# Folding w_out in four column groups, 32-row tiles for the last keys of the small attention, six staging slots

## The chip, the cores and the metric

One core of one Trainium2 chip runs the kernel. The metric is device time in microseconds, the median of several runs. Most runs of this kernel lie within 0.3% of each other.

## The reference, cut to what matters

Three stages follow each other. The sizes are 4 batches, 8 heads, 576 positions, head size 64; 2304 tokens of 512; 1536 hidden columns; 8 experts with 4 slots each.

```
q_d, k_d, v_d = means over 4 neighbouring positions          # 144 positions
out  = repeat(softmax_attention(q_d, k_d, v_d), 4) + local_attention(q, k, v)   # |i - j| < 4
x    = out as (2304, 512)
x    = (x @ w_a) * (x @ w_b) @ w_out                          # w_a, w_b: 512 x 1536, w_out: 1536 x 512
logits = x @ phi                                              # phi: 512 x 32
slots  = softmax(logits, over tokens).T @ x                   # 32 x 512
y[e]   = relu(slots[e] @ w1[e]) @ w2[e]                       # 8 experts
return softmax(logits, over slots) @ y
```

w_a, w_b and w_out arrive as float64 words and become float32 on the chip.

## The kernel before, in words

The x of the second stage is never multiplied by w_out token by token. The kernel **folds** w_out into phi first (w_out @ phi, 1536 x 32) and takes logits from the gated product; w_out itself is applied later to the 32 slots. The attention is worked out batch by batch: the **small attention** over the 144 pooled positions (`plan_datt`), and the local attention in pairs of 116 positions (`plan_pair`), whose output is split in a high and a low part (`xhi`, `xlo`) for the **main matmuls** (`plan_unit`, line 1086). These go over five groups of 384 or 512 tokens; a group has 12 units, a unit two halves (w_a and w_b), and a half 12 matmuls: four blocks of 128 rows, three products each.

**Weights.** `plan_piece` brings one piece of w_a, w_b or w_out (512 KB of words) into a staging slot, makes its low bits (`clow`), magnitude (`mag`) and bits (`bits`), and for w_a and w_b the high and low parts (`chi`, `clo`). Two pieces make one weight tile, which serves two units. The first `FIRST` = 20 pieces use the four slots named `st`, the later ones the two slots named `sw`. The `st` slots are taken out of the 24 places named `w8`, and all are given back when the last of the `FIRST` pieces is done. A weight tile takes two `w8` places.

**Folding.** A piece of w_out.T holds 128 of the 512 columns of w_out and 512 hidden rows. `omm` (line 947) folds two pieces in one task: a piece is one matmul of 32 x 512 into its own 32 partitions of `ps`. After four pieces, `e1` copies the 128 x 512 result to SBUF and `e2` (line 1046) adds the four groups of 32 partitions and turns them, in four matmuls; `e3` copies them to `wpr`. That is done for three blocks of hidden rows (fc = 0, 1, 2).

**Small attention.** `dscore`, `dmax`, `dexp`, `dnorm` and `dptr` (lines 673, 686, 701, 293, 733 to 740) make the transposed weights in three parts: two parts of four heads with the first 128 keys, and one with the last 16 rows. The last 16 keys of all eight heads are kept in one tile, `dvr`, of 8 x 16 = 128 rows; a head's columns in it are zero outside its own 16 rows. `dout(n)` (line 779) makes the output of four heads: for each of two column halves two matmuls over the first 128 keys, then two over all 128 rows of `dvr`. `doev` copies it, and `pv` and `xadd` of the batch's pairs need it.

**Order.** The programme of every engine is written out by hand: `ORDER` lists all tasks, `OTHER` those that go to their second engine. A task is a closure with one or a few instructions. Engines take their tasks strictly in that order, so an engine that waits holds up all that stands behind it. Loads are all issued by SP, in order too. Idle times of TensorE that the order foresees are filled with matmuls on constants (lines 347 and 352).

Of the kernel before, what the change touches and what calls it, by code (L numbers as in the profile page):

```python
# [9 lines left out]
F32 = mybir.dt.float32  # L10
# [238 lines left out]
def tile_attn_glu_softmoe(  # L249
# [16 lines left out]
    nc = tc.nc  # L266
    ctx.enter_context(tc.manual_schedule())
    P = Plan(dict(CAPS))
    add = P.add
# [338 lines left out]
    def plan_datt(b):  # L608
# [163 lines left out]
        def dout(n):  # L772
            pt = X.pop(("pt", b, n))
            X["do", b, n] = ps = psum((128, 2, 144))
            for hl in range(2):
                for part in range(2):
                    for j in range(2):
                        h = 4 * n + 2 * j + hl
                        nc.tensor.matmul(  # L779
                            out=ps[j * 64:j * 64 + 64, hl, :],  # L780
                            lhsT=(X["dvr", b] if part else X["dv", b])[:, h, :],
                            rhs=X["pr", b] if part else pt[:, 2 * j + hl, :],
                            start=(part == 0),
                            stop=(part == 1),
                        )
            if n == 0:
                done_with(PT_AT[b], X.pop(("ptr", b)))
            if n == 1:
                X.pop(("dv", b))
                X.pop(("dvr", b))  # L790
                X.pop(("pr", b))
# [37 lines left out]
        for n in (2, 0, 1):  # L829
# [6 lines left out]
            if n == 1:  # L836
# [8 lines left out]
                alt=("V", 0.85 if n < 2 else 0.8, WT["norm"]), lk=0.0, gi=2,  # L845
# [14 lines left out]
            T["pt", b, n] = t6  # L860
        for n in range(2):
            o = pr + 0.2 + 0.1 * n
            t7 = add(
                "PE", 1.05, lambda n=n: dout(n), [T["pt", b, n]] + tb + vv + T["xd", b] + T.get(("dout", b), []), o - 40,
                acq=("ps",) if n else ("ps", "xd"), rel=("dpt", "dv", "dvr", "dpr") if n else (PT_AT[b],), part="128x64",
            )
            T.setdefault(("dout", b), []).append(t7)
            T["xd", b].append(
                add("A", 0.4, lambda n=n: doev(n), [t7] + T["xd", b], o, rel=("ps",))
            )  # L870

# [30 lines left out]
    def plan_piece(n, key):  # L902
# [39 lines left out]
        def omm():  # L942

            if ("wp", fc) not in X:
                X["wp", fc] = psum((128, 512))
            for x in range(m - OQ + 1, m + 1):
                nc.tensor.matmul(  # L947
                    out=X["wp", fc][x * 32:x * 32 + 32, :], lhsT=phis[:, x, :],
                    rhs=words(X["raw", (fc, x)])[0].bitcast(F32), start=True, stop=True,
                )  # L950
# [16 lines left out]
        if isw:  # L967
            t5 = add(
                "A", 0.57, chi, [t4, T.get(("chi",) + key[:3]), T.get("chi0") if m == 0 else None], o - 0.01, acq=("w8", "w8") if m == 0 else (), alt=("G", 0.62, WT["chi"])
            )  # L970
            T["chi", *key[:3]] = t5
            if m == 0:
                T["chi0"] = t5
            t7 = add("G", 1.3, clo, [t5], o - 1, alt=("V", 0.63, WT["clo"]), lk=0.0)
            part.append(t7)
            T.setdefault(("w",) + key[:3], []).append(t7)
        else:
            T.setdefault(("ocv", fc), []).append(t4)
            if m % OQ == OQ - 1:
                if m == OQ - 1:  # L980
                    T["lg", fc] = add("N", 0.0, lambda: None, [t4], -100, acq=("lg", "ps"), lat=0.0)
                t7 = add("PE", 0.95, omm, T["ocv", fc][m - OQ + 1:] + [t_phi, T["lg", fc]], o - 20, part="128x32")
                T.setdefault(("omm", fc), []).append(t7)
                for x in range(m - OQ + 1, m):
                    T["conv"].append(add("N", 0.0, lambda x=x: X[where].append(X.pop(("raw", (fc, x)))), [t7], 0, rel=(where,), lat=0.0))
                part += [t7]
            else:
                return
# [48 lines left out]
    def plan_wprime(fc):  # L1037
        def e1():
            X["wT", fc] = sb(at, "dpt", (128, 4, 144)).rearrange("p a b -> p (a b)")[:, 0:512]
            nc.scalar.copy(out=X["wT", fc], in_=X.pop(("wp", fc)))  # L1040

        def e2():
            X["wq", fc] = ps = psum((128, 4, 32))
            wT = X.pop(("wT", fc))
            for fi in range(4):
                nc.tensor.matmul(
                    out=ps[:, fi, :], lhsT=wT[:, fi * 128:fi * 128 + 128], rhs=rep32, start=True, stop=True
                )
# [7 lines left out]
        t = add("A", 0.58, e1, T["omm", fc], -5, acq=("dpt",), rel=("ps", "lg"))  # L1056
        t = add("PE", 0.92, e2, [t, t_cst], -45, acq=("ps",), rel=("dpt",))
# [563 lines left out]
OQ = 2  # L1621
# [6 lines left out]
FIRST = 20  # L1628
# [3 lines left out]
def cpr(c):  # L1632
# [122 lines left out]
```

## Time and profile before

| | |
|---|---|
| median of 3 runs | 488.15 us (487.72 to 488.18) |
| profiled execution | 489.66 us, of which its span 487.9 us |
| PE busy | 470.3 us (96%) |
| DVE, ACT, POOL busy | 270.0, 153.3, 118.7 us |
| main matmuls, line 1086 | 1440, 56% of the chain that ended last |
| granted TensorE clock | 0.994 |
| DMA | 84.26 MB, mean 173 GB/s |

PE is TensorE, DVE is VectorE, ACT is ScalarE, POOL is GpSimd, SP issues the loads. The span is the time from the first to the last instruction; the profiled execution's own time is 1.8 us longer. PE is nearly always busy, so a PE instruction that is left out shortens the span, unless something else is late. In the first 80 us some of the busy time is filler; in the last 15 us the output leaves.

### The profile page before, as it was taken

Reading aid. Unit: us, or ns where it says so; the run is one execution under the profiler, and the core shown is the slowest. Engines: PE = TensorE matmul, PEld = TensorE weight load, DVE = VectorE, ACT = ScalarE, POOL = GpSimd, SP = SyncE. Lnnn points to the kernel's source line nnn. Section 1 sums busy time; section 2 is a strip of 40 time slices with the busy share of each in tenths; the row PEclk is TensorE's granted clock in tenths of the full one; section 3 lists DMA queues with packets and bytes.
Section 4 is the critical chain, followed back from the end, with each engine's and each line's share of the span. In section 5 each row is a group of like instructions: output and inputs, shape, how many; then the busy total and the mean of one; then the engine's idle time right before and its main releaser. Section 6 shows DMA issues by size and latency. Waiting matters only on the chain.

```text
span 487.9 us, 11280 instructions
## 1 busy us (share of the span) xinstructions
PE 470.3 (96%) x4702; PEld 366.5 (75%) x4702; DVE 270.0 (55%) x561; ACT 153.3 (31%) x403; POOL 118.7 (24%) x181
## 2 busy tenths in 40 slices
PE   8989988999999999999999999999999999999992
PEld 4678978987777687778788777778878889853471
DVE  4889899675654943686534237623332735660131
ACT  2876666342233521220152201302030301130142
POOL 6887787110540210633130002200000000010000
PEclk9999999999999999999999999999999999999997
DMA  8987862344444100413001010033223778999997
GB/s 297 385 279 238 294 192 93 124 172 155 165 153 154 46 0 27 131 64 125 3 22 45 1 39 28 24 118 119 87 86 130 263 257 313 401 364 411 407 406 287
DMA packets 30402, 84.26 MB, mean 173 GB/s; under 512 B 3472, under 2 KB 4240, under 8 KB 30352
## 3 DMA queue, kind: packets, MB, share of 16 engines
q1 hardware_dynamic: 30352, 83.54, 47.9%
q8 instruction: 37, 0.61, 0.5%
q14 instruction: 13, 0.11, 0.1%
HBM read 78.81 MB, written 4.72 MB: 171 GB/s over the span
## 4 chain that ended last, share of the span: by engine, by line
PE 83%; ACT 0%; DVE 0%; DVEq 0%; issue 0%
PE ps L1086 56%; PE ps L1246 3%; PE ps L1508 3%; PE ps L1455 3%; PE ps L1111 3%; PE ps L530 2%; PE ps L779 1%; PE ps L516 1%; PE ps L947 1%; PE ps L472 1%; PE ps L1547 1%; PE ps L673 1%; PE ps L1163 1%; PE ps L352 1%; PE ps L733 1%; PE ps L1414 1%
## 5 line engine op out<-in xcount | busy, mean ns | idle before, releaser
L1086 PE MATMUL ps<-x,w 128*128 128x512 f32 (+1 forms) x1440 | 307.5, 371 | 1.0 <-DVE x L293 0.9
L1086 PEld LDWEIGHTS ps<-x,w 128*128 128x128 f32 x1440 | 260.2, 188 | 46.1 <-issue 9.1
L1101 DVE TENSOR_TENSOR gr<-a,ps 128x512 f32<-128x512 f32 (+1 forms) x60 | 37.8, 629 | 82.4 <-PE ps L1086 73.8
L288 ACT COPY a<-ps 128x512 f32<-128x512 f32 (+1 forms) x35 | 19.3, 556 | 89.9 <-PE ps L1086 89.9
L293 POOL TENSOR_TENSOR x<-xn,x 128x464 fp32r<-128x464 f32 (+4 forms) x16 | 17.4, 1094 | 89.2 <-ACT x L288 83.7
L1119 DVE STREAM_TRANSPOSE gr<-gr 128x1024 f32<-128x1024 f32 (+2 forms) x31 | 33.1, 1086 | 9.2 <-PE ps L1111 9.2
L1233 POOL TENSOR_TENSOR cn<-lc,cs 128x128 f32<-128x128 f32 (+1 forms) x5 | 1.9, 377 | 119.3 <-DVE cs L1230 74.9
L290 DVE COPY a<-ps 128x384 f32<-128x384 f32 (+1 forms) x25 | 15.1, 603 | 20.7 <-PE ps L1086 20.7
L541 DVE TENSOR_TENSOR xn<-ps,xd 128x232 f32<-128x232 f32 (+1 forms) x40 | 13.8, 388 | 13.6 <-PE ps L530 13.4
L347 PE MATMUL ps<-acc 128*128 128x512 f32 (+2 forms) x44 | 16.8, 513 | 3.5 <-POOL acc L340 2.2
L293 POOL TENSOR_TENSOR w<-w,w 128x512 fp32r<-128x512 f32 x14 | 19.1, 1373 | 0.6
L293 POOL TENSOR_TENSOR e<-e,mx 128x512 f32<-128x512 f32 x12 | 12.5, 1045 | 27.0 <-DVE mx L506 27.0
L499 ACT ACTIVATE e<-e 128x512 f32<-128x512 f32 x20 | 12.6, 632 | 17.9 <-DVE e L492 17.8
L480 DVE TENSOR_REDUCE mx<-ps 128x4 f32<-128x256 f32 x40 | 14.7, 415 | 6.1 <-PE ps L472 6.1
L430 POOL TENSOR_TENSOR dT<-dT,qk 128x116 f32<-128x116 f32 (+1 forms) x34 | 17.4, 512 | 2.7
L288 ACT CAST x<-xn 128x464 fp32r<-128x464 f32 (+5 forms) x17 | 8.9, 532 | 27.7 <-DVE xn L541 27.7
L530 PEld LDWEIGHTS ps<-e,bv 64*64 64x64 f32 x640 | 12.4, 133 | 5.6 <-issue 3.4
L1246 PE MATMUL ps<-gr,lgs 32*32 32x384 f32 x576 | 16.4, 491 | 0.0
L892 ACT ACTIVATE ps<-w8x 128x512 f32<-128x512 f32 x12 | 7.6, 638 | 26.7 <-DVE a L290 13.3
L892 ACT ACTIVATE ps<-sw 128x512 f32<-128x512 f32 x16 | 10.1, 631 | 17.0 <-DMA sw<-in_w_outt_dram 11.1
L347 PEld LDWEIGHTS ps<-acc 128*128 128x128 f32 x44 | 8.4, 208 | 9.3 <-issue 6.6
L492 DVE TENSOR_TENSOR e<-ps,mx 128x256 f32<-128x256 f32 x40 | 14.7, 416 | 0.0
(205 smaller groups left out, 589.5 us busy)
## 6 DMA issues: line engine op xcount, KB each, us to landing
w<-in_moe_w_dram SPq DMA_DIRECT2D x33, 512.0 KB, 7.2
qk<-in_qk_dram SPq DMA_DIRECT2D x17, 480.0 KB, 4.8
sw<-in_w_outt_dram SPq DMA_DIRECT2D x12, 512.0 KB, 4.2
w8x<-in_moe_w_out_dram SPq DMA_DIRECT2D x12, 512.0 KB, 3.9
w<-in_moe_w_a_dram SPq DMA_DIRECT2D x10, 512.0 KB, 5.6
w<-in_moe_w_b_dram SPq DMA_DIRECT2D x10, 512.0 KB, 4.9
bv<-in_vw_dram SPq DMA_DIRECT2D x20, 256.0 KB, 3.8
w8x<-in_moe_w_dram SPq DMA_DIRECT2D x10, 512.0 KB, 10.3
```

The costliest lines, as they stand in the source:

```text
L288: nc.scalar.copy(out=out, in_=in_)
L290: (nc.vector if e == "V" else nc.gpsimd).tensor_copy(out=out, in_=in_)
L293: (nc.vector if e == "V" else nc.gpsimd).tensor_tensor(**a)
L347: nc.tensor.matmul(out=X["warm"][:, 0:128 * w], lhsT=x[:, 0:128], rhs=x[:, 0:128 * w], start=True, stop=True)
L430: nc.gpsimd.tensor_tensor(out=dst, in0=dst, in1=one[r], op=ALU.add)
L480: nc.vector.tensor_reduce(out=mx[:, hl], in_=X["s", n, hl], op=ALU.max, axis=AX.X)
L530: nc.tensor.matmul(out=pss[hl][o:o + 64, hq // 2, bi * w:bi * w + w], lhsT=v[r, bi, hq, :], rhs=pt[r, hq, 1 + bi * 64:1 + bi * 64 + w], st ...
L892: nc.scalar.activation(out=f, in_=words(raw)[0].bitcast(F32), func=ACTF.Prelu, scale=2.0 ** -112, alpha=-(2.0 ** 32))
L1086: nc.tensor.matmul(out=ps, lhsT=X["w", fc, ab, fi // 2, wi][:, fi % 2, hq, :], rhs=X[x, g][:, hq, :], start=(hq == 0 and m == 0), stop=(hq ...
L1101: nc.vector.tensor_tensor(out=X["g", g][:, k, :], in0=X.pop(("a", g, k)), in1=X.pop(("mm", g, k, 1)), op=ALU.mult)
L1119: nc.vector.transpose(out=t, in_=t)
L1246: nc.tensor.matmul(out=ps[q][o:o + 32, :], lhsT=d[r, b, :], rhs=g[r, :, b * 32:b * 32 + 32], start=(b < 4), stop=(b >= gt // 32 - 4),)
```

## The change

`omm` folds one piece in a task of its own: four matmuls of 128 columns, one to each group of 32 partitions, and the four pieces of a block are added up in `ps` while they come. `e1` then copies 128 x 128, and `e2` is one transpose. `dout` of a batch is one task instead of two, and its second parts take only the 32 rows of `dvr` and `pr` that two heads share. The `st` slots are six and `FIRST` is 18. `ORDER` and `OTHER` are new throughout (1328 tasks instead of 1326).

```
-        def dout(n):
-            pt = X.pop(("pt", b, n))
-            X["do", b, n] = ps = psum((128, 2, 144))
+        def dout():
+            pts = [X.pop(("pt", b, n)) for n in range(2)]
+            pss = [psum((128, 2, 144)) for _ in range(2)]
+            v, w, q = X.pop(("dv", b)), X.pop(("dvr", b)), X.pop(("pr", b))
             for hl in range(2):
                 for part in range(2):
-                    for j in range(2):
-                        h = 4 * n + 2 * j + hl
-                        nc.tensor.matmul(
-                            out=ps[j * 64:j * 64 + 64, hl, :],
-                            lhsT=(X["dvr", b] if part else X["dv", b])[:, h, :],
-                            rhs=X["pr", b] if part else pt[:, 2 * j + hl, :],
...
+                    for n in range(2):
+                        X["do", b, n] = pss[n]
+                        for j in range(2):
+                            h = 4 * n + 2 * j + hl
+                            r = slice(64 * n + 32 * j, 64 * n + 32 * j + 32)
+                            nc.tensor.matmul(
+                                out=pss[n][j * 64:j * 64 + 64, hl, :], lhsT=w[r, h, :] if part else v[:, h, :],
+                                rhs=q[r, :] if part else pts[n][:, 2 * j + hl, :], start=(part == 0), stop=(part == 1),
+                            )
...
         def omm():
-            if ("wp", fc) not in X:
-                X["wp", fc] = psum((128, 512))
-            for x in range(m - OQ + 1, m + 1):
+            if m == 0:
+                X["wp", fc] = psum((128, 128))
+            w = words(X["raw", key])[0].bitcast(F32)
+            for y in range(4):
                 nc.tensor.matmul(
-                    out=X["wp", fc][x * 32:x * 32 + 32, :], lhsT=phis[:, x, :],
-                    rhs=words(X["raw", (fc, x)])[0].bitcast(F32), start=True, stop=True,
+                    out=X["wp", fc][y * 32:y * 32 + 32, :], lhsT=phis[:, m, :], rhs=w[:, y * 128:y * 128 + 128],
+                    start=(m == 0), stop=(m == 3),
                 )
...
         def e2():
             X["wq", fc] = ps = psum((128, 4, 32))
-            wT = X.pop(("wT", fc))
-            for fi in range(4):
-                nc.tensor.matmul(
-                    out=ps[:, fi, :], lhsT=wT[:, fi * 128:fi * 128 + 128], rhs=rep32, start=True, stop=True
-                )
+            nc.tensor.transpose(out=ps.rearrange("p a b -> p (a b)"), in_=X.pop(("wT", fc)), identity=ident)
...
-OQ = 2
-FIRST = 20
+FIRST = 18
-    ps=8, un=2, lg=2, st=4, sw=2, ...
+    ps=8, un=2, lg=2, st=6, sw=2, ...
```

**Start-up, the queue of loads (SP).** `qk` and `x` are the queries and keys of the pairs (`x` where they lie in spare room), `cst` and `xn` constants, `w_87` and so on the staging slots, `sw` the two late slots, `bv` and `gr` values. Before:

```order
L413 DMA qk<-in_qk_dram 128x960
L370 DMA cst<-const_dram 128x269
L367 DMA xn<-const_dram 128x192
L413 DMA qk<-in_qk_dram 128x960
L413 DMA x<-in_qk_dram 128x960 x2
L913 DMA w_87<-in_moe_w_a_dram 128x2x256
L413 DMA x<-in_qk_dram 128x960
L652 DMA bv<-in_vr_dram 128x256
```

In the change:

```order
L413 DMA qk<-in_qk_dram 128x960 x2
L367 DMA xn<-const_dram 128x192
L370 DMA cst<-const_dram 128x269
L413 DMA x<-in_qk_dram 128x960 x3
L904 DMA w_143<-in_moe_w_a_dram 128x2x256
L652 DMA bv<-in_vr_dram 128x256
```

All five pairs of the first batch are now loaded ahead of the first piece of weights.

**The folding on PE, at the first block's end.** L1086 (now L1068) are main matmuls, L947 (L939) is `omm`, L1046 (L1030) is `e2`, L462 and L516 belong to the local attention. Before:

```order
L1086 MATMUL ps<-x,w_866 128x512 x2
L1086 MATMUL ps<-x,w_867 128x512
L1046 MATMUL ps<-cst,dpt 128x32 x4
L947 MATMUL ps<-sw,phis 32x512 x2
L462 LDWEIGHTS eyeb
```

In the change:

```order
L516 MATMUL ps<-cst,e 128x128 x4
L1030 MATMUL ps<-cst,dpt 128x128
L939 MATMUL ps<-sw,phis 32x128 x4
L1068 MATMUL ps<-x,w_997 128x512 x2
L1068 MATMUL ps<-x,w_998 128x512
```

A task of two matmuls of 512 columns is now one of four of 128 columns, and there are twelve of them instead of six.

**The small attention's output on PE, batch 1.** `gr` and `dpt` hold the transposed weights of the first and the second four heads. Before, the first of two tasks:

```order
L516 MATMUL ps<-cst,e 128x128 x8
L779 MATMUL ps<-gr,dv 64x144 x2
L779 MATMUL ps<-dpr,dvr 64x144 x2
L779 MATMUL ps<-gr,dv 64x144 x2
L779 MATMUL ps<-dpr,dvr 64x144 x2
L1086 MATMUL ps<-x,w_1024 128x384 x2
```

In the change, the only one:

```order
L516 MATMUL ps<-cst,e 128x128 x4
L784 MATMUL ps<-gr,dv 64x144 x2
L784 MATMUL ps<-dpt,dv 64x144 x2
L784 MATMUL ps<-dpr,dvr 64x144 x4
L784 MATMUL ps<-gr,dv 64x144 x2
L784 MATMUL ps<-dpt,dv 64x144 x2
L784 MATMUL ps<-dpr,dvr 64x144 x4
L1068 MATMUL ps<-x,w_1058 128x384 x2
```

The 16 matmuls of a batch stand together, in four runs that change between 128 and 32 rows.

## Rows read from the trace of the kernel before

**Rows 1.** Windows: us, busy time (instructions) of PE, PEld, DVE, ACT, POOL; clock, DMA share, GB/s.

```profile
60.00:80.00 20.00, 17.07 (x108) 15.76 (x107) 19.29 (x35) 13.80 (x37) 15.01 (x18) 1.00 0.42 133
80.00:100.00 20.00, 20.00 (x223) 17.95 (x224) 13.65 (x28) 8.11 (x22) 6.21 (x8) 1.00 0.46 145
...
440.00:470.00 30.00, 30.00 (x429) 14.60 (x429) 2.68 (x9) 4.41 (x10) 0.00 (x0) 1.00 1.03 408
```

**Rows 2.** Timeline of PE at start-up: start, length, what, idle before and its releaser.

```profile
40.23 2.18 PE L1086 MATMUL ps<-x,w 128*128 128x384 f32 x11 [0.91 <-DVE x L293]
...
63.21 0.44 PE L733 MATMUL ps<-cst,gr 128*128 128x128 f32 x2 [1.56 <-POOL gr L293]
...
74.48 0.63 PE L733 MATMUL ps<-cst,gr 128*128 128x128 f32 x4 [1.37 <-DVE gr L293]
```

**Rows 3.** The chain that ended last, in order of time: start, us, what, records.

```profile
75.11 0.11 PE ps L737
...
91.81 1.13 PE ps L779 x16
...
98.00 1.02 PE ps L947 x4
...
118.90 0.81 PE ps L1046 x8
...
155.58 0.41 PE ps L673 x16
155.98 1.01 PE ps L1046 x8
...
186.56 2.94 PE ps L1086 x12
...
293.48 13.83 PE ps L1086 x60
...
465.59 1.01 PE ps L1508 x32
```

**Rows 4.** Timelines of PE, SP's queue and DVE at start-up.

```profile
14.64 1.76 PE L673 MATMUL ps<-dT,dT 64*32 64x144 f32 x32
...
27.99 0.72 PE L530 MATMUL ps<-e,bv 64*64 64x58 f32 x30
...
28.83 1.87 SPq L452 DMA_DIRECT2D bv<-in_vw_dram  x2
...
34.88 0.74 PE L530 MATMUL ps<-e,bv 64*64 64x58 f32 x32
...
38.80 1.29 DVE L293 TENSOR_TENSOR x<-xn,x 128x144 fp32r<-128x144 f32 x1
```

**Rows 5.** Timelines of SP's queue, ACT, DVE and POOL ahead of the wait at 63.21.

```profile
51.44 0.38 SPq L913 DMA_DIRECT2D w<-in_moe_w_b_dram  x1
...
58.28 0.67 ACT L886 ACTIVATE w<-w 128x512 uint32<-128x512 uint32 x1 [1.90 <-DMA w<-in_moe_w_b_dram]
...
61.11 0.17 DVE L709 RECIPROCAL dm<-dm 128x2 f32<-128x2 f32 x1
...
61.63 1.52 POOL L293 TENSOR_TENSOR gr<-gr,dm 128x128 f32<-128x128 f32 x2
```

**Rows 6.** Timelines of DVE and POOL, 40 to 80 us.

```profile
40.01 0.68 DVE L503 TENSOR_REDUCE mx<-e 128x8 f32<-128x520 f32 x1
...
79.82 0.45 DVE L686 TENSOR_REDUCE dn<-ps 128x2 f32<-128x288 f32 x1
...
66.30 1.31 POOL L293 TENSOR_TENSOR w<-w,w 128x512 fp32r<-128x512 f32 x1
```

**Rows 7.** SP's queue and PE in the tail (timelines), and DMA issues: KB, us to landing.

```profile
462.63 2.88 SPq L1361 DMA_DIRECT2D gr<-in_moe_w_dram  x3
...
474.64 1.64 PE L1508 MATMUL ps<-gr,acc 128*32 128x128 f32 x48
...
gr<-in_moe_w_dram SPq DMA_DIRECT2D x10, 512.0 KB, 8.2
```

More of the change, by code (lines that the diff above doesn't have):

```diff
@@ L770, in drest @@
                 X.pop(("dr", b))
-        def dout(n):
-            pt = X.pop(("pt", b, n))
-            X["do", b, n] = ps = psum((128, 2, 144))
+        def dout():
+            pts = [X.pop(("pt", b, n)) for n in range(2)]
+            pss = [psum((128, 2, 144)) for _ in range(2)]
+            v, w, q = X.pop(("dv", b)), X.pop(("dvr", b)), X.pop(("pr", b))
             for hl in range(2):
                 for part in range(2):
-                    for j in range(2):
-                        h = 4 * n + 2 * j + hl
-                        nc.tensor.matmul(
-                            out=ps[j * 64:j * 64 + 64, hl, :],
-                            lhsT=(X["dvr", b] if part else X["dv", b])[:, h, :],
-                            rhs=X["pr", b] if part else pt[:, 2 * j + hl, :],
-                            start=(part == 0),
-                            stop=(part == 1),
-                        )
[L786 to L791, printed above, removed]
+                    for n in range(2):
[7 more added lines that the diff above has]
+                            )
+            done_with(PT_AT[b], X.pop(("ptr", b)))
         def doev(n):
@@ L844, in plan_datt @@
                 "G", 1.38 if n < 2 else 1.22, lambda e, n=n: dnorm(n, e), [t4], o, rel=("dm",),
-                alt=("V", 0.85 if n < 2 else 0.8, WT["norm"]), lk=0.0, gi=2,
+                alt=("V", 1.3, WT["norm"]), lk=0.0, gi=2,
             )
@@ L860, in plan_datt @@
             T["pt", b, n] = t6
+        t7 = add(
+            "PE", 1.6, dout, [T["pt", b, 0], T["pt", b, 1]] + tb + vv, pr + 0.3 - 40,
+            acq=("ps", "ps", "xd"), rel=("dpt", "dv", "dvr", "dpr", PT_AT[b]), part="128x64",
+        )
         for n in range(2):
[L862 to L867, printed above, removed]
             T["xd", b].append(
-                add("A", 0.4, lambda n=n: doev(n), [t7] + T["xd", b], o, rel=("ps",))
+                add("A", 0.4, lambda n=n: doev(n), [t7] + T["xd", b], pr + 0.2 + 0.1 * n, rel=("ps",))
             )
@@ L977, in plan_piece @@
         else:
[L978 to L988, printed above, removed]
+            if m == 0:
+                T["lg", fc] = add("N", 0.0, lambda: None, [t4], -100, acq=("lg", "ps"), lat=0.0)
+            t7 = add("PE", 0.32, omm, [t4, t_phi, T["lg", fc]] + T.get(("omm", fc), [])[-1:], o - 20, part="128x32")
+            T.setdefault(("omm", fc), []).append(t7)
+            part += [t7]
         t = add("N", 0.0, lambda: X[where].append(X.pop(("raw", key))), part, 0, rel=(where,), lat=0.0)
@@ L1038, in e1 @@
         def e1():
-            X["wT", fc] = sb(at, "dpt", (128, 4, 144)).rearrange("p a b -> p (a b)")[:, 0:512]
+            X["wT", fc] = sb(at, "dpt", (128, 4, 144)).rearrange("p a b -> p (a b)")[:, 0:128]
             nc.scalar.copy(out=X["wT", fc], in_=X.pop(("wp", fc)))
@@ L1043, in e2 @@
             X["wq", fc] = ps = psum((128, 4, 32))
-            wT = X.pop(("wT", fc))
-            for fi in range(4):
-                nc.tensor.matmul(
-                    out=ps[:, fi, :], lhsT=wT[:, fi * 128:fi * 128 + 128], rhs=rep32, start=True, stop=True
-                )
+            nc.tensor.transpose(out=ps.rearrange("p a b -> p (a b)"), in_=X.pop(("wT", fc)), identity=ident)
         def e3():
@@ L1054, in e3 @@
                 nc.scalar.copy(out=phis, in_=view(ps, [[0, 4], [1, 32]], 96))
-        t = add("A", 0.58, e1, T["omm", fc], -5, acq=("dpt",), rel=("ps", "lg"))
-        t = add("PE", 0.92, e2, [t, t_cst], -45, acq=("ps",), rel=("dpt",))
+        t = add("A", 0.25, e1, T["omm", fc], -5, acq=("dpt",), rel=("ps", "lg"))
+        t = add("PE", 0.2, e2, [t, t_cst], -45, acq=("ps",), rel=("dpt",))
         T["conv"].append(t)
@@ L1639 @@
 ORDER = [
[61 rows of a table removed]
[62 rows of a table added]
 ]
 OTHER = [
[8 rows of a table removed]
[7 rows of a table added]
 ]
 CAPS = dict(
-    ps=8, un=2, lg=2, st=4, sw=2, w8=24, qk=2, bv=2, mx=4, e=3, xn=2, x=2, cps=2, dv=1, dT0=1, dT1=1, dn=3, dm=3,
+    ps=8, un=2, lg=2, st=6, sw=2, w8=24, qk=2, bv=2, mx=4, e=3, xn=2, x=2, cps=2, dv=1, dT0=1, dT1=1, dn=3, dm=3,
     dr=1, dpt=1, dvr=1, dpr=1, ost=2, xd=1, a=2, ht=2, lgs=1, nm=3, al=3, sm=3, L=3, cm=3, lc=2,
```

138 rows, old and new, of tables (ORDER, OTHER) are left out of this document.

## The prediction, made before the changed kernel was run

> **What bounds the kernel now.** I read the windows first. From 80 us until the last weights PE is busy all the time: 20.00 of 20 us, 30.00 of 30 [rows 1]. There, a microsecond of PE work that is left out is a microsecond of time, unless a transfer or another engine then comes too late. Before 80 us it is different: between 60 and 80 us PE has 17.07 us and DVE 19.29 [rows 1]. So I read PE's timeline for the first 80 us. The main matmuls can go on only at 40.23, after 0.91 us of idle time for DVE's last low part of x, and then PE stands twice more, 1.56 us for POOL and 1.37 us for DVE, both times in front of a transpose of the small attention of batch 1 [rows 2]. After that it never stands again before the tail. The time is therefore the start of the main matmuls, plus the waits behind it, plus the PE work that is left, plus a tail that changes little. In both orders the same tasks stand ahead of the first main matmul. The chain of waits gives the price of each PE task in the busy stretch [rows 3].
>
> **The change on PE, term by term.** All durations are from the profiled execution (span 487.9, its time 489.66 us), and the sum is made against that; the median of the runs is 488.15, 1.5 us under the profiled time, and I move it by the same amount.
>
> *Folding.* Six tasks of 1.02 us go, 6.1 us (the row at 98.00) [rows 3]. Twelve tasks of four matmuls of 128 columns in four column groups come. The nearest row is the experts' second layer, the same shape: 16 such matmuls in 1.01 us, 0.25 us for four (at 465.59) [rows 3]. A task that stands alone costs more. What breaking a stream costs is seen in the main matmuls: twelve alone take 2.94 us, sixty in a row 13.83, 2.77 for twelve [rows 3], so 0.17 us. Twelve times 0.42 is 5.0 us: **1.1 us less**. The ends are 0.25 us a task (3.1 us less) and half of the old task, 0.51 (nothing).
>
> *Turning the fold.* Three tasks of 0.81, 0.81 and 1.01 us go (at 118.90 and 155.98; the one at 153.15 reads as the first) [rows 3]. One transpose of 128 x 128 takes 0.11 us inside a task (at 75.11) [rows 3]; with 0.17 for the break it is 0.28, three times 0.8. **1.8 us less**; 2.3 without the break, and 1.3 if each costs four transposes (0.44).
>
> *The small attention's output.* Two tasks of 1.13 us go a batch, eight matmuls each (at 91.81) [rows 3]. The eight matmuls over the first 128 keys keep their shape and cost 1.13. The eight over the last keys now use 32 rows, in four tiles of the array instead of two. The trace before has no 32 x 64 tile. The nearest row is the small attention's last scores: eight matmuls of the same 144 columns in 64 x 32 tiles take 0.41 us (at 155.58) [rows 3]. With four tiles instead of eight I take half of 1.13, 0.57. The task has four runs of shapes; I add two breaks of 0.17. That is 2.04 instead of 2.26 us, **0.7 us less** for the three batches in the busy stretch (batch 0 lies in the start-up). The ends: 1.70 a batch (1.7 us less), and 2.60 if the 32-row tiles bring nothing (1.0 us more). No row of this trace shows two row tiles that write the same bank of PSUM. In the new code the matmuls of j = 0 and j = 1 do just that. The Trainium skill says against it (TensorEngine Tiling, Restrictions and Gotchas) that different row tiles cannot use one PSUM bank at the same time. No run here has shown this yet; that case is the third rival below.
>
> Together 3.6 us less on PE (between 7.1 and 0.3 less). The copies on ACT that become smaller (`e1`, 128 x 512 to 128 x 128) cost nothing on the path: ACT is busy 8 us of 20 there [rows 1]. Should they run late, only the transposes behind them wait.
>
> **The start.** The small attention of batch 0 begins when all five pairs have landed and are pooled: scores at 14.64. Its output leads to the first product with the values at 27.99, this frees a buffer for the next values (issued 28.83, first used 34.88), and the last low part of x is done at 40.1 [rows 4]. The order puts the fifth pair's load ahead of the first 512 KB of weights, some 1.3 us at the 408 GB/s that the tail reaches [rows 1], and gives DVE seven of the ten poolings that were shared five and five. Against it: DVE has as many tasks up to that low part as before (48 or 49), so little of a gain upstream may reach it. I take **1.0 us less**; the ends are 2.5 less (the transfer, and the filler ahead of the scores) and 1.0 more.
>
> **The waits.** The 1.56 us at 63.21 can be followed back: POOL's scaling at 61.63 follows DVE's reciprocal at 61.11, and ACT came late to the exponentials because it stood 1.90 us until 58.28 for a piece of weights that SP could issue only at 51.44, when a staging slot came free [rows 5]. Eight slots (six and two) instead of six let two more pieces be on their way, so this cause should go. What is late next is the scaling itself: the order leaves the same distance, two half units, between those scores and their transpose. I count half of that wait, **0.8 us less**; the ends are both waits gone (2.9 less) and 3 more, by the first rival.
>
> Sum: 3.6 + 1.0 + 0.8 = 5.4 us. Span 482.5, profiled execution 484.3, median 488.15 - 5.4 = **482.7 us**. A measurement of this kernel tells about 0.2% (1 us) from no change.
>
> **The rivals.** *First: the weight conversion becomes the bound.* Six `st` slots leave 18 places for nine weight tiles, so the last three tiles can be filled only when all 18 first pieces are done. By the order, DVE has 38 tasks from x's last low part to there, and 24 more to the bits of the second piece of the tile that holds w_b of units 8 and 9. Before, DVE did 58 tasks from 40.01 to 80.2, 0.69 us each [rows 6]: 62 tasks are 42.9 us, and a cast and a subtraction on POOL (1.31 [rows 6] and about half of that) make 44.9. PE comes there after 18 half units of about 2.2 us [rows 2] and some 5 us of attention work, 44.7 us. That is just in time. One to 3 us late gives 484 to 486 us: 16%. *The slower end* is the same mechanism from 6.4 us late on, ten tasks of delay on DVE or two loads that wait for slots in turn: 489 us or more. Against it, before the change DVE kept such a pace without a wait of PE for weights. 6%.
>
> *Second: the tail takes it back.* The expert weights come at 408 GB/s between 440 and 470 us with the DMA share at 1.03 [rows 1], and the last are issued from 462.63 to 465.5, land 8.2 us later and are used from 474.64 on [rows 7]: 1 to 3 us of slack. If the stream can't begin earlier, the gain ends there: 485 to 487.5 us. Against it, its loads wait for places that the main matmuls free, and these move forward too. 10%, half of it within the bound of no change.
>
> *Third: the 32-row tiles go two at a time.* The last keys of a batch then take as long as before, 1.13 us, and the breaks come on top: 1.0 us more instead of 0.7 less, 484.4 us. This is what the skill's rule named above would make of it. 8%.
>
> That the change doesn't do what it says is not open: the order shows the transposes, the twelve tasks and the loads where they should be.
>
> **How the numbers follow.** The forecast, 480 to 484, has 58%; the first rival 16, the second 10, the third 8, slower 6, and 2 are left for a start that gains more than 2.5 us. The range 479.0 to 487.0 leaves out the slower end, half of the second rival and the last 2. Faster by over 0.2% is 58 + 16 + 5 + 8 + 2, less 1 for a conversion 5 us late: 88. Same 6, slower 6.
>
> **What would show it.** Right: fold tasks near 0.4 us and turns under 0.3 in the chain, an output task near 2.0, main matmuls from about 39 us, less than 2.9 us of waits between there and 80 us, and PE full until the tail. Wrong: PE waiting for DVE or POOL in front of a main matmul near 80 us (first rival), PE waiting for DMA after 440 us (second), an output task of 2.6 us (third).

## The result: 482.02 us, and the profile after

The changed kernel takes 482.02 us (median of 4 runs, 481.27 to 482.39); the kernel before, run beside it, 487.94 (487.28 to 488.18). The ratio is **0.9879** (95% interval 0.9862 to 0.9896), so 5.9 us are gone where 5.4 were forecast. The profiled execution took 482.01 us, its span is 480.2. One execution each of two later variants was disturbed (1591.55 us with less output, 583.13 with the folds in pairs), and the ratios below leave them out.

The windows that answer to [rows 1], with one more from the tail (same columns):

```profile
60.00:80.00 20.00, 19.13 (x135) 17.66 (x134) 16.58 (x34) 9.71 (x30) 14.46 (x16) 1.00 0.39 122
80.00:100.00 20.00, 20.00 (x232) 18.39 (x232) 12.96 (x27) 10.49 (x30) 8.94 (x9) 1.00 0.53 166
440.00:470.00 30.00, 30.00 (x484) 15.87 (x480) 5.47 (x16) 7.13 (x18) 0.00 (x0) 1.00 1.03 407
470.00:475.00 5.00, 3.37 (x78) 2.38 (x70) 1.53 (x4) 2.38 (x9) 0.00 (x0) 1.00 0.93 367
```

From 80 us on PE is still full, but for a wait of 0.30 us near 395, and between 60 and 80 it has 19.13 us instead of 17.07. The start of its main matmuls and its waits from there to the tail, in its timeline (the rows answer to [rows 2]):

```profile
39.38 10.47 PE L1068 MATMUL ps<-x,w 128*128 128x384 f32 x59 [0.92 <-DVE x L293]
...
64.83 0.48 PE L673 MATMUL ps<-dT,dT 64*32 64x144 f32 x16 [0.62 <-DVE dT L425]
...
69.93 0.41 PE L733 MATMUL ps<-cst,gr 128*128 128x128 f32 x2 [0.25 <-DVE gr L293]
...
395.53 1.68 PE L1068 MATMUL ps<-x,w 128*128 128x384 f32 x8 [0.30 <-ACT a L288]
```

The waits of 1.56 and 1.37 us [rows 2] have become 0.62 and 0.25. The chain of waits gives the new price of the tasks that the change touches (start, us, what, records; they answer to [rows 3]):

```profile
89.33 2.09 PE ps L784 x32
...
123.32 0.11 PE ps L1030
123.43 0.36 PE ps L939 x8
126.76 0.36 PE ps L939 x8
...
146.09 0.59 PE ps L939 x16
147.67 0.11 PE ps L1030
```

A fold task (line 939) is 0.36 us, two that stand together 0.59, a turn (line 1030) 0.11, the small attention's output of a batch (line 784) 2.09.

The span can be cut in four on PE's timeline: the start of the main matmuls; PE's work from there to the end of its last matmul; its waits in between, those of the last microseconds included; and what comes after the last matmul.

| profile | main start | PE work | waits | last matmul | tail | span |
|---|---|---|---|---|---|---|
| before | 40.23 | 435.6 | 3.3 | 479.1 | 8.8 | 487.9 |
| after | 39.38 | 432.8 | 2.1 | 474.3 | 5.9 | 480.2 |
| difference | -0.85 | -2.8 | -1.2 | -4.8 | -2.9 | -7.7 |

These two executions lie 7.7 us apart and the medians 5.9, since the profiled one of before was 1.5 us above its median. A second profile of before (the last experiment) shows which of the four parts that concerns.

### The profile page after: what moved, and what is told of

Its sections match the earlier page's. It is cut to its first block, busy times and chain, and to the rows that moved or that the text cites. A ratio compares the mean times of both kernels' runs of the same rounds, so it can differ in the third digit from the quotient of the medians.

```text
span 480.2 us, 11383 instructions
## 1 busy us (share of the span) xinstructions
PE 466.8 (97%) x4755; PEld 363.0 (76%) x4755; DVE 269.4 (56%) x570; ACT 145.4 (30%) x392; POOL 121.6 (25%) x180
## 4 chain that ended last, share of the span: by engine, by line
PE 84%; DVE 7%; ACT 4%; DMA 3%; issue 1%; SPq 0%; POOL 0%; ACTq 0%; DVEq 0%; POOLq 0%
PE ps L1068 58%; PE ps L1490 3%; PE ps L1437 3%; PE ps L1228 3%; PE ps L1093 3%; PE ps L530 2%; DMA w<-in_moe_w_dram 2%; PE ps L516 2%; DMA x<-in_qk_dram 1%; PE ps L784 1%; PE ps L673 1%; PE ps L472 1%; DVE dT L425 1%; PE ps L1529 1%; ACT ps L883 1%
## 5 line engine op out<-in xcount | busy, mean ns | idle before, releaser
L1068 PE MATMUL ps<-x,w 128*128 128x512 f32 (+1 forms) x1440 | 308.5, 371 | 1.2 <-DVE x L293 0.9
L1068 PEld LDWEIGHTS ps<-x,w 128*128 128x128 f32 x1440 | 259.8, 188 | 43.6 <-issue 5.5
L293 POOL TENSOR_TENSOR x<-xn,x 128x464 fp32r<-128x464 f32 (+4 forms) x12 | 13.1, 1091 | 84.4 <-DVE x L290 73.6
L290 DVE COPY a<-ps 128x512 f32<-128x512 f32 (+1 forms) x22 | 14.1, 643 | 19.4 <-PE ps L1068 19.4
L293 POOL TENSOR_TENSOR w<-w,w 128x512 fp32r<-128x512 f32 x16 | 21.0, 1327 | 2.8 <-ACT w L288 2.5
L1228 PE MATMUL ps<-gr,lgs 32*32 32x384 f32 x576 | 16.3, 491 | 0.1
L425 DVE TENSOR_REDUCE dT<-qk 128x116 f32<-128x464 f32 (+1 forms) x20 | 12.0, 620 | 6.1 <-DMA qk<-in_qk_dram 6.1
L430 POOL TENSOR_TENSOR dT<-dT,qk 128x116 f32<-128x116 f32 (+1 forms) x28 | 14.7, 524 | 2.2
L530 PE MATMUL ps<-e,bv 64*64 64x58 f32 (+1 forms) x640 | 14.9, 226 | 0.1
L883 ACT ACTIVATE ps<-sw 128x512 f32<-128x512 f32 x18 | 11.4, 633 | 11.0 <-DVE xn L541 4.8
```

Of the source, the lines that this page charges most:

```text
L293: (nc.vector if e == "V" else nc.gpsimd).tensor_tensor(**a)
L425: nc.vector.tensor_reduce(out=dst, in_=view(src, dims, off), op=ALU.add, axis=AX.X)
L430: nc.gpsimd.tensor_tensor(out=dst, in0=dst, in1=one[r], op=ALU.add)
L530: nc.tensor.matmul(out=pss[hl][o:o + 64, hq // 2, bi * w:bi * w + w], lhsT=v[r, bi, hq, :], rhs=pt[r, hq, 1 + bi * 64:1 + bi * 64 + w], st ...
L883: nc.scalar.activation(out=f, in_=words(raw)[0].bitcast(F32), func=ACTF.Prelu, scale=2.0 ** -112, alpha=-(2.0 ** 32))
L1068: nc.tensor.matmul(out=ps, lhsT=X["w", fc, ab, fi // 2, wi][:, fi % 2, hq, :], rhs=X[x, g][:, hq, :], start=(hq == 0 and m == 0), stop=(hq ...
```

## The experiments

**Fold and turn alone.** The order of before, with only the two new forms:

```
-            X["wp", fc] = psum((128, 512))
+            X["wp", fc] = psum((128, 128))
...
+                w = words(X["raw", (fc, x)])[0].bitcast(F32)
+                for y in range(4):
                     nc.tensor.matmul(
-                        out=X["wp", fc][x * 32:x * 32 + 32, :], lhsT=phis[:, x, :], ...
+                        out=X["wp", fc][y * 32:y * 32 + 32, :], lhsT=phis[:, x, :],
+                        rhs=w[:, y * 128:y * 128 + 128], start=(x == 0), stop=(x == 3),
...
-            for fi in range(4): ...
+            nc.tensor.transpose(out=ps..., in_=X.pop(("wT", fc)), identity=ident)
```

> The kernel before with its own order; only the folding and the turning are the new ones (eight matmuls of 128 columns a task in six tasks, a copy of 128 x 128, one transpose). Theory (PE work in the busy stretch moves the time one for one): fold tasks of 0.6 us as the pair in the changed kernel took 0.59, so 6 x 0.43 = 2.6 us less, and 2.3 us less for the three turns: 4.9 us less than before, about 483.0. Rival (the gain needs the new order, since what PE would reach earlier is not ready): waits of PE between 80 and 430 us or in the tail that take half or more of it back, 485.5 or more.

Measured: 484.33 us, ratio 0.9932 (0.9908 to 0.9955), 3.3 us less: short of the 4.9 that the theory gave, more than the rival allowed. PE's work falls from 435.6 to 431.4, all of it in these rows of its chain, where two pieces are 0.59 us and not 1.02, and a turn 0.11 to 0.26:

```profile
95.67 0.59 PE ps L949 x16
...
148.51 0.11 PE ps L1046
148.62 0.59 PE ps L949 x16
150.21 0.26 PE ps L1046
```

The rival's waits are not there: between 80 and 430 us PE waits once, 0.28 us. The profiled execution was 0.7 us faster than the median of its runs; beyond that, why PE's 4.2 us give 3.3 is open. So more than half of the gain is the new forms by themselves, and they need no new order. But PE's work is 1.5 us *smaller* here than in the changed kernel, though the latter also has the shorter output of the small attention; and the tail is 9.0 us, about as before. The new order, with its slots, costs PE work and gains in the tail.

**The turn made longer again.** The changed kernel with four matmuls of 32 columns ahead of each transpose:

```
+            for fi in range(4):
+                nc.tensor.matmul(out=ps[:, fi, :], lhsT=wT, rhs=rep32, start=True, stop=True)
             nc.tensor.transpose(out=ps..., in_=wT, identity=ident)
```

> The changed kernel with four matmuls of 32 columns, the work of the old turn, ahead of each of the three transposes; the result is not touched by them. Theory (one for one): three times about 0.75 us, 2.2 to 2.4 us more, 484.3. Rival (slack behind it, in the waits near 395 us or in the tail, takes it up): 1 us more or less than that.

Measured: 484.38 us, ratio 0.9933 (0.9912 to 0.9954), 2.4 more than the changed kernel. A turn goes from 0.11 to 0.95 us in the chain (0.81 for the four matmuls and 0.14 for the transpose), three times 0.84 are 2.5. This PE work in the busy stretch costs its own length.

**All 128 rows for the last keys.** The changed kernel, still one task a batch:

```
-  lhsT=w[r, h, :] if part else v[:, h, :], rhs=q[r, :] if part else ...
+  lhsT=w[:, h, :] if part else v[:, h, :], rhs=q if part else ...
```

> The changed kernel, only that the second parts of the small attention's output go over all 128 rows again. Theory (four 32-row tiles work at once, although two of them write one bank): the runs of four second-part matmuls go from 0.40 to about 0.6 us less one break, an output task from 2.09 to about 2.3, three in the busy stretch, 0.3 to 0.8 us more: 482.3 to 482.8. Rival (the 32-row tiles take turns and the gain of the task lies in the joining of its halves): a task of 2.1 or less and no difference.

Measured: 482.22 us, ratio 0.9881 (0.986 to 0.9901): no difference from the changed kernel. The 32 rows bring nothing, as the rival had it, but not because the tiles take turns. PE's timeline of the first half of the task and the start of the second (start, length, records; a matmul leaves two records, and a step lasts until the next begins), the changed kernel first:

```profile
89.26 0.47 PE L784 MATMUL ps<-gr,dv 128*64 128x144 f32 x4
89.56 0.41 PE L784 MATMUL ps<-dpt,dv 128*64 128x144 f32 x4
89.91 0.47 PE L784 MATMUL ps<-dpr,dvr 32*64 32x144 f32 x8
90.31 0.47 PE L784 MATMUL ps<-gr,dv 128*64 128x144 f32 x4
```

and with 128 rows:

```profile
89.36 0.47 PE L784 MATMUL ps<-gr,dv 128*64 128x144 f32 x4
89.65 0.41 PE L784 MATMUL ps<-dpt,dv 128*64 128x144 f32 x4
89.90 0.66 PE L784 MATMUL ps<-dpr,dvr 128*64 128x144 f32 x8
90.39 0.42 PE L784 MATMUL ps<-gr,dv 128*64 128x144 f32 x4
```

With 128 rows the second step takes 0.25 us and the third, of four matmuls, 0.49. With 32 rows the third takes 0.40, but the second 0.35: what the narrow tiles save, 0.09, is lost where the shape changes. The task is 2.11 us with 128 rows and 2.09 with 32; the 0.15 us that a batch still gains with 128 rows over two tasks of 1.13 comes from joining the halves, the only other difference of the task.

**The 32 rows with the halves apart.** The kernel before, where only j = 0 and j = 1 can then work together, and these write one bank:

```
-  lhsT=(X["dvr", b] if part else X["dv", b])[:, h, :], rhs=X["pr", b] if part else ...
+  lhsT=X["dvr", b][r, h, :] if part else X["dv", b][:, h, :], rhs=X["pr", b][r, :] if part else ...
```

> The kernel before, the small attention's output still in two tasks a half batch, but its last keys in 32 rows: then the only two 32-row tiles that can work together, j = 0 and j = 1, write one PSUM bank. Theory (row tiles may share a bank): the four matmuls of a second part take about 0.24 to 0.3 us as in 128 rows, the task 1.1 to 1.3. Rival (they take turns): 0.48 or more for four, a task of 1.6 us, 1.5 us more for the three batches in the busy stretch.

Measured: 492.72 us in one run, span 490.9. A task is 1.57 us instead of 1.13, the price that I had put to tiles that take turns. But PE's timeline shows another cause (x4 are two matmuls of two records each, one pair; a second part of the expectation is two such pairs):

```profile
86.21 0.47 PE L780 MATMUL ps<-gr,dv 128*64 128x144 f32 x4
86.61 0.46 PE L780 MATMUL ps<-dpr,dvr 32*64 32x144 f32 x4
87.00 0.47 PE L780 MATMUL ps<-gr,dv 128*64 128x144 f32 x4
87.39 0.46 PE L780 MATMUL ps<-dpr,dvr 32*64 32x144 f32 x4
```

Every step takes 0.39 to 0.40 us, the pairs in 128 rows, which write different column groups, no less than those in 32 rows. Turns would have lengthened the 32-row pairs alone, to 0.48 (twice the 0.24 of an unbroken pair) and a break on top. What all four steps share is the change of shape at their ends: 0.15 us each over the 0.24. Neither of the two expectations held; the break was the term missing in both. Six such tasks in the busy stretch are 2.6 us more, near the 2.9 that PE's work gains on the first profile of before (438.5 for 435.6); the rest of this single execution is mostly its late start, 40.95.

**Four and five staging slots.** The changed kernel with fewer slots and the same order on every engine:

```
-    ps=8, un=2, lg=2, st=6, sw=2, ...
+    ps=8, un=2, lg=2, st=4, sw=2, ...
```

> The changed kernel with four st slots instead of six; every engine keeps its tasks in the same order, so loads wait longer for a slot and more room is left for weight tiles. Theory (the waits of PE in the start-up went because more pieces are on their way): main matmuls later by 0.5 to 3 us and PE's waits between there and 90 us 1 to 4 us longer, 483.5 to 489. Rival (the order alone did it): start and waits within 0.5 us of the changed kernel, 482.0.

> The changed kernel with five staging slots instead of six, the same order on each engine. With four it lost 14.4 us: SP stood for a slot from 12.3 to 21.3 and from 33.8 to 43.7, what is queued behind came late, and PE waited 5.8 us and started 4.2 us late. Theory (each slot less holds back all the loads behind it on SP): part of that, 484 to 490 us, with the main matmuls starting after 40 and over 3 us of waits before 80. Rival (only the last two slots together matter, since weights come in pairs): 482.0.

Measured: 496.44 us with four (ratio 1.0178, 1.0154 to 1.0201) and 485.31 with five (0.994, 0.992 to 0.9959), 14.4 and 3.3 us more than with six. The four-slot run is far above what I expected. SP's queue shows why:

```profile
11.93 0.34 SPq L452 DMA_DIRECT2D bv<-in_vw_dram  x1
21.34 0.37 SPq L904 DMA_DIRECT2D w<-in_moe_w_a_dram  x1
...
33.82 9.89 SPq L904 DMA_DIRECT2D w<-in_moe_w_b_dram  x2
43.75 0.47 SPq L904 DMA_DIRECT2D sw<-in_moe_w_b_dram  x1
```

SP stands for a slot for nine microseconds, twice, and the attention's own loads stand behind it. In the windows (columns as above) the DMA engines move 158 and 15 GB/s in the first two of these, where the changed kernel has 387 and 261:

```profile
20.00:25.00 5.00, 4.14 (x28) 2.97 (x28) 4.96 (x11) 4.62 (x15) 4.29 (x7) 1.00 0.50 158
...
40.00:45.00 5.00, 4.02 (x97) 3.52 (x90) 4.09 (x9) 4.06 (x8) 3.86 (x4) 1.00 0.13 15
...
70.00:75.00 5.00, 3.06 (x12) 2.58 (x12) 4.20 (x11) 3.23 (x6) 1.32 (x1) 0.81 0.97 372
75.00:80.00 5.00, 1.66 (x19) 1.25 (x20) 4.56 (x9) 2.15 (x6) 4.63 (x4) 0.50 0.03 11
80.00:85.00 5.00, 5.00 (x22) 5.00 (x21) 4.22 (x8) 1.95 (x7) 4.13 (x6) 0.66 0.79 259
```

The main matmuls begin at 43.6, and PE waits 2.38 us until 71.81 and 3.47 until 78.34, both times for DVE, which has itself stood 5.91 us for a late piece of weights with the attention's tasks behind it:

```profile
69.32 0.43 DVE L879 TENSOR_SCALAR w<-w 128x512 uint32<-128x512 uint32 x1 [5.91 <-DMA w<-in_moe_w_b_dram]
...
71.81 3.06 PE L1068 MATMUL ps<-x,w 128*128 128x384 f32 x12 [2.38 <-DVE e L492]
78.34 0.73 PE L673 MATMUL ps<-dT,dT 64*32 64x144 f32 x16 [3.47 <-DVE dT L425]
```

Behind the first wait the granted clock falls to the lower of its levels, 1.2 GHz (0.50 in the stretch from 75 to 80), and it is at 1.00 again from 85 us on. Twelve main matmuls take 3.06 us at 71.81, where they take 2.38 elsewhere, and all of them together are 2.7 us longer in this run; another 2.8 us of PE's work are filler that this variant has among them, from 47.71 on. With five slots the same things happen smaller: the start is at 40.6, ACT stands 3.36 us for a piece until 62.96, PE waits 2.1 us for DVE until 68.78, and the granted clock is 0.50 from 69 to 72. So this order needs its six slots. It does not say that two slots more would have given 14 us to the order of before, which was made for four.

**Four more fold tasks in pairs.** The changed kernel with tasks moved in the order only:

```
 fold (0,1) moved to just before fold (0,2); (0,3) before (1,0); (1,1) before (1,2); (2,0) before (2,1)
```

> The changed kernel with four of the twelve fold tasks moved behind later ones, so that four more pairs stand together (as one pair does now, 0.59 us for eight matmuls where two single tasks take 0.73) and two main streams are broken less. Theory (a new order's side cost is its breaks): PE work 0.8 to 1.0 less, 481.1 us. Rival 1 (the stream of expert weights and outputs sets the end): PE work less, time 482.0. Rival 2: the later fold holds its staging place longer, PE waits for weights, 483 or more.

Measured: 485.86 us, ratio 0.9951 (0.9933 to 0.997), 3.8 more than the changed kernel. That is the second rival. Fold work falls by 0.3 us, but PE's timeline has two new waits, 3.2 us together:

```profile
102.39 0.67 PE L939 MATMUL ps<-sw,phis 128*32 128x128 f32 x16
...
119.31 0.30 PE L462 MATMUL ps<-band,eyeb 64*64 64x256 bf16 x2 [1.03 <-ACT dpt L1026]
...
129.33 0.65 PE L939 MATMUL ps<-sw,phis 128*32 128x128 f32 x8 [2.18 <-DVE sw L888]
```

and SP's queue shows where the second comes from:

```profile
115.78 8.56 SPq L909 DMA_DIRECT2D sw<-in_w_outt_dram  x2
```

and in the changed kernel:

```profile
115.32 4.31 SPq L909 DMA_DIRECT2D sw<-in_w_outt_dram  x2
```

There are two `sw` places. A piece's fold gives its place back, and only then can SP issue the next load. The second of these two loads is issued at 124.0 (0.33 us before the row's end), behind the pair of folds at 123.5; in the changed kernel, where a fold stands alone at 118.8, at 119.3. The first wait has a late load behind it as well: ACT, whose copy PE waits for, stood 6.04 us for a piece of w_out until 117.91. Behind the second the granted clock is 0.50 from 129.33 to 132.33, and the main matmuls are 0.8 us longer in this run, so that PE's work is 0.6 more and not 0.8 less. The single tasks of the change, which cost more PE time than pairs, return each place as soon as they can.

**Fewer breaks.** Three fold tasks moved where the trace leaves room:

```
 fold (0,0) moved before pv(5); (0,1) before (0,2); (1,1) before pv(8)
```

> The changed kernel with three fold tasks moved: the first and the sixth ahead of the product with the values beside them, so that the two 64-row tasks around each stand together (0.51 us instead of 0.67), the second behind 12 main matmuls to the third (a pair, one break less, 0.38 us less in the run with four pairs). All three weight tiles are converted in time by the trace of the changed kernel (ends at 90.2, 99.2 and 116.3). Theory (a break costs its 0.15 to 0.4 us as long as no staging place is held longer than its next load can bear): PE work 0.7 less, no new wait, 481.3 us. Rival (any later fold starves the loads, as in the run with four pairs): over 1 us of new waits between 100 and 136, 483 or more.

Measured: 482.46 us, ratio 0.9881 (0.985 to 0.9912). PE work is 0.4 us less, not 0.7, there are no new waits between 100 and 136, and in this execution the wait for ACT near 395 is 0.98 instead of 0.30. The time does not differ from that of the changed kernel by more than the runs of either do: neither the 481.3 of the theory nor the rival's 483 is shown.

**Less output.** Half of each block of the first 256 output columns is not stored, in the fold-alone kernel (two runs, the second for its trace) and in the changed one:

```
-  m = (n - n0 + 1) * 288
+  m = (n - n0 + 1) * (144 if d0 < 256 else 288)
```

> The kernel before with the new fold and turn alone, and of the first 256 columns of the output only half of each block is stored (1.18 MB of output is left out). Theory: in the order of before the tail is bound by the backlog of transfers. The DMA engines are full until 476.5 in the fold-alone run, its last matmul is done at 472.8 and the span ends 9.0 us later. 1.18 MB at 408 GB/s are 2.9 us: about 481.5 us (2.4 to 2.9 less than the 484.3 of the fold alone, ratio near 0.987), with some 6.3 us from the last matmul to the end. Rival: the tail is the last copies and the fixed latency of the last store; then 484.3 (ratio 0.993).

> The fold alone with 1.18 MB of output left out, once more, for its trace. Theory of the backlog: the DMA engines are done earlier after the last matmul than in the fold-alone run, 6 to 6.6 us from the last matmul's end to the end of the span, where the fold alone has 9.0; rival: 9.0 again.

> The changed kernel with the same 1.18 MB of output left out. Theory: in the changed kernel the backlog is gone before the last matmuls (its DMA rate falls to 230 GB/s from 474 to 475.5), so the end is the last matmul, its copies and one store: 481.2 to 482.0 us, at most 0.8 less than 482.0. Rival (the tail of both kernels is the transfers): 2.9 less, 479.1.

Measured: for the fold alone a ratio of 0.9861 (0.9828 to 0.9894) where it had 0.9932, 3.5 us less (2.2 by the medians, 482.15 for 484.33), and in the second run, of 480.95 us, 6.3 us from the last matmul to the end instead of 9.0. For the changed kernel 481.1 us, 0.9 less by the median, 1.5 by the ratios (0.9849, 0.9823 to 0.9875), more than the 0.8 that I expected at most, and half of the rival's 2.9 or less. The stretches after the last matmul, the fold alone first:

```profile
472.80:474.80 2.00, 0.00 (x0) 0.00 (x0) 1.12 (x3) 0.71 (x3) 0.00 (x0) 1.00 1.03 404
474.80:476.80 2.00, 0.00 (x0) 0.00 (x0) 0.00 (x0) 0.00 (x0) 0.00 (x0) 0.87 1.03 404
476.80:478.80 2.00, 0.00 (x0) 0.00 (x0) 0.00 (x0) 0.00 (x0) 0.00 (x0) 0.50 0.70 275
```

and the changed kernel (nothing left out):

```profile
474.30:476.30 2.00, 0.00 (x0) 0.00 (x0) 0.45 (x2) 1.42 (x5) 0.00 (x0) 1.00 0.78 306
476.30:478.30 2.00, 0.00 (x0) 0.00 (x0) 0.00 (x0) 0.00 (x0) 0.00 (x0) 0.75 1.01 391
478.30:480.30 2.00, 0.00 (x0) 0.00 (x0) 0.00 (x0) 0.00 (x0) 0.00 (x0) 0.50 0.10 38
```

In the fold-alone run a backlog of some 2.2 MB is left when the last matmul ends (the three rates times 2 us), and the DMA engines stay full for 4 us; in the two profiles of before it is 2.1 and 1.9 MB. In the changed kernel it is 1.5 MB, and the engines are not full while the last copies are made. So in the order of before the tail is bound by the transfers: what was left out came through whole, within the noise. In the changed kernel a third to a half of it did, so there the transfers bind in part and the last matmul with its copies for the rest.

**Before, once more.** The unchanged kernel, for a second profile.

> The kernel before, unchanged, for a second profile. The fold-alone run, in which the order ahead of the main matmuls is that of before, began its main matmuls at 38.48 where the profiled run of before began at 40.23. Theory (the start differs between executions by more than the change gives): main matmuls from 38.3 to 39.8 here and a span near 486. Rival (the profiled start of before is typical): 40.0 to 40.4.

Measured: 488.3 us, span 486.5. The main matmuls begin at 39.19, there are 0.54 and 1.35 us where [rows 2] have 1.56 and 1.37, PE works 435.9 us, all its waits from the start on are 3.1 us, the tail is 8.4:

```profile
39.19 2.17 PE L1086 MATMUL ps<-x,w 128*128 128x384 f32 x11 [0.92 <-DVE x L293]
...
61.16 0.44 PE L733 MATMUL ps<-cst,gr 128*128 128x128 f32 x2 [0.54 <-POOL gr L293]
```

So the start and the first wait differ by 1 us between executions of the same kernel; PE's work and the tail hardly do.

## Why the prediction was right, and where its terms were not

The time, 482.02 for 482.7, came as forecast. The mechanism, PE work in a full stretch and shorter waits before it, is what the runs show, but several terms were off and in part made up for each other. The terms, against the sum's own:

- **Folding: right in kind, too small.** I had 1.1 us less, from 0.42 us a task. A single task is 0.36 and the one pair 0.59, together 4.2 us instead of 6.1: 1.9 less. The step that failed is the 0.17 us for a broken stream, taken from main matmuls; 0.11 over the 0.25 is what it cost here.
- **Turning: too small.** I had 1.8 us less, from 0.28 a turn. It is 0.11, with no break at all, 2.3 less for the three (2.63 to 0.33 in the chain). The longer turn shows that this counts one for one.
- **The small attention's output: 0.5 us less, not 0.7, and for another reason.** I got 2.04 us a batch by halving the second part in 32-row tiles; it is 2.09, but the run with 128 rows has 2.11. The breaks cost about what the tiles gave. The gain is that of one task instead of two, which I had costed at nothing. The step that failed is the break, put at two times 0.17: each change of shape cost 0.10 to 0.16 here, and there are four.
- **The rule on row tiles and banks.** The third rival rested on the Trainium skill (TensorEngine Tiling, Restrictions and Gotchas: different row tiles cannot use one PSUM bank at the same time). The traces do not bear it out for these tiles, which lie in different column groups as well: a pair of 32-row tiles on one bank takes 0.39 us, as does the pair in 128 rows beside it, and four of them, two to a bank, take 0.40 in the changed kernel, where two turns of 0.24 would be 0.48. The third rival's output task of 2.6 us and its time, 484.4, did not come.
- **The new order on PE: missing.** I had no term for what the order does to other work on PE. The direct terms are 4.7 us, PE's work fell by 2.8. The rest, 1.9, is in work that the change does not touch, by line before and after, each record counted until the next begins: the products with the values (line 530) 9.3 and 10.1 us, the main matmuls 303.1 and 303.8 (in 37 unbroken stretches and in 40), the task `new` (line 1311, now 1293) 1.22 and 1.75; the smaller differences nearly cancel. The last of the three is no break: its neighbours are the same fillers in both kernels, and its fourth part begins only when DVE's last copy of `acc`, which the new order puts behind a weight task, is done (429.3 us). In the fold-alone run, in the old order, all three stayed as they were. The run with fewer breaks moved three tasks and took 0.24 us from line 530 alone; that breaks explain the rest of the first two is argued and not shown.
- **The start: not shown.** I had 1.0 less. The five profiles in the order of before begin at 38.5 to 40.9 us (mean 39.7), the six in the new order with six slots at 38.6 to 39.7 (39.2): 0.4 us between the means, less than executions of one kernel differ. The gain upstream is there and is lost on the way: the scores come 0.85 us earlier than in [rows 4], the first product with the values 0.08.

```profile
13.79 1.76 PE L673 MATMUL ps<-dT,dT 64*32 64x144 f32 x32
...
27.91 0.72 PE L530 MATMUL ps<-e,bv 64*64 64x58 f32 x30
```

- **The waits: right in kind.** I had 0.8 less. Between the start and 80 us PE waited 2.9 and 1.9 us in the two profiles of before and 0.9 in the changed kernel. What I called late next, the scaling, is late by 0.25; the larger one, 0.62, is a wait of the scores (line 673) for DVE, which I had not named. New waits come later, 0.30 us near 395 and 0.55 in the last microseconds, so that all waits together are 1.2 and 1.0 us less. The cause that I gave, pieces issued late for want of a slot, is borne out by the runs with fewer slots, where SP stands for a slot, ACT or DVE for the piece and PE for the attention's task behind it.
- **The tail: wrong.** I called it a tail "that changes little". It was 8.4 to 9.0 us in four profiles of the old order with all of its output, and is 5.9 to 6.7 in seven of the new one. The second rival looked at this place and feared the opposite, that the stream of weights would eat the gain. Relative to PE's end the stream is ahead: SP has issued the last expert weights 13.6 us before the last matmul's end in before and 16.3 us in the changed kernel. That is about 1.1 MB at 408 GB/s, against the 0.4 to 0.7 MB of backlog that are missing. That the order's earlier loads do this is read from the queue; no run moved these loads alone.

Against the first and the second profile of before, the changed kernel's profile has: start -0.85 and +0.2, PE's work -2.8 and -3.1, waits -1.2 and -1.0, tail -2.9 and -2.4; together -7.7 and -6.3, while the medians differ by 5.9. The forecast of 5.4 had 3.6, 1.0 and 0.8 and nothing for the tail. Its direct terms on PE were 1.1 too small and it put the order's cost of 1.9 at nothing; the 1.0 of the start is not shown; and the tail, put at nothing, gave more than two microseconds. That these errors nearly cancelled is luck.

The first rival did not come: with six slots PE's waits in the start-up are 0.62 and 0.25 us, and neither stands in front of a main matmul. Slots do bound this order, but from the other side: one slot less costs 3.3 us and two cost 14.4, not because a weight tile lacks room but because pieces are issued late. The second rival, PE waiting for DMA after 440 us, did not come either.

## What to carry to other kernels

Cost a new order like an edit: count where it splits runs of one tile shape, 0.1 to 0.2 us each in this kernel, and look at what an earlier or later task gives back, since a task that is cheaper in a pair can hold a staging place that the next load needs. In a stretch where PE and the DMA engines are both full, compare what is left to transfer when the last matmul ends; work removed from PE comes through only as far as that backlog does not grow by it. Take two profiles before a difference of a microsecond in the start-up is explained.

## What the runs showed that I had not expected

Narrowing a matmul's rows from 128 to 32 changed nothing in the time of a task whose four narrow tiles work together, and made a task 0.44 us longer where only two could: each change between 128-row and 32-row tiles cost 0.15 us there, more than the narrow tiles gave. Waits of PE of 2.10, 2.18 and 2.38 us, in three runs, were each followed by a stretch at a granted clock of 0.50, and the main matmuls of these runs were 0.9, 0.8 and 2.7 us longer on top of the waits. And two staging slots fewer cost 14.4 us, because SP, which issues all loads in order, stood for nine microseconds twice with the attention's loads behind it.
